# Scaling the second copy of the values on GpSimd instead of VectorE

## The chip, the cores and the metric

The kernel runs on one core of a Trainium2 chip. The core has five engines, each with a queue of its own that it works through in order: TensorE (PE, with its weight loads as PEld), VectorE (DVE), ScalarE (ACT), GpSimd (POOL) and SyncE (SP, which issues DMAs). They wait for one another through semaphores. The metric is the time of one execution on the device, in microseconds (us).

## What is computed

Two branches share one normalised input, and both are added to x:

```python
xn = layernorm(x)                              # x: 1 x 2048 x 512, bf16
# A: attention with 32 heads of 16 columns
q, k, v = split(xn @ wqkv)
p = softmax(q @ k.T * 16 ** -0.5)              # 2048 x 2048 for each head
a = (p @ v) @ wo
# B: an MLP over the token axis
u = gelu(einsum("bsd,sf->bdf", layernorm(xn), w1) + b1)
y = (einsum("bdf,fs->bds", u, w2) + b2).transpose
return x + a + y
```

## The kernel before

The work of attention is cut into 32 blocks: 4 blocks of 512 queries (qb) by 8 groups of 4 heads. For each block, PE makes scores for 16 tiles of 128 keys, 4 heads at once in four row groups of the array, into banks of PSUM (`ps`). The exponential of the scores is made in two ways, tile by tile:

- ScalarE takes the exponential of a bank into `pT` (`exp_tile`, L775).
- Or VectorE turns the score into a 16-bit integer whose bits, read as bf16, are a rough exponential (`first_planes`, L839). Two more such integers, shifted by constants, are derived from it, and the three, read as bf16, are summed by PE to a finer exponential. The three are called planes. The second and third plane are an add of one constant to four 16-bit integers at a time, done by GpSimd as a 64-bit integer add (`make_plane`, L849, `INT64_ADD` in the profile), in a few cases by VectorE. The planes lie in `planes` and, once their first contents are no longer needed, in `x_sb`, `xn_sb`, `xnT` and `w2blk`. One such region is up to four tiles of 512 columns.

The product with the values (`pv_mm`, L787) takes an exponential or a plane as its moving operand and 17 columns for each head of the values as weights: 16 of values and one of ones, which gives the softmax's denominator. The first of the three planes has the weight 0.75 (`WEIGHT[0]`). So the values are held twice: `V17` with the values and the ones, and `V17b`, the same times 0.75, which is used with first planes alone. (The profile's names leave numbers out: `V` is V17, `V17b` stays.)

The values are made in 19 pieces (`v_steps`): one piece of 4 key tiles and six of 2 for the first 8 heads (T = 0), four of 4 key tiles for the next 8 (T = 1), eight of 2 key tiles for the last 16 (T = 2 and 3). For each piece PE multiplies, VectorE copies the result from PSUM into V17 (`v_evac`, L692, `CAST V<-ps`), and `v_scale` (L750) writes the piece of V17b. A piece is 544 columns on 128 partitions, in six cases 272.

The order of all work is written out by hand as a text of codes (`ORDER`) and replayed into one list for each engine; each operation waits for the writers of what it reads and for the readers of what it overwrites. `sc.add("dve", ...)` appends to VectorE's list, `sc.add("pool", ...)` to GpSimd's. The place of a piece's scaling in the text is a few steps behind its copy. Before its first integer add GpSimd has memsets alone: constants, zeros of V17b and of parts of `QT` and `gT`.

## Time and profile before

| | |
|---|---|
| median of 3 runs | 627.7 us (627.61 to 628.27) |
| the profiled execution | 627.96 us, span 626.2 us |
| PE busy | 617.4 us (99%) |
| ACT busy | 614.1 us (98%) |
| DVE busy | 584.3 us (93%) |
| POOL busy | 430.6 us (69%) |
| granted TensorE clock | 1.0 |

The span is the time from the first to the last record of the program on the core; the execution's own time is 1.8 us longer. Busy shares are means over all stages. In the lists below, a row of a queue gives the start and the length in us, the engine, the source line, the operation, what it writes and reads, and in brackets the idle time of the engine ahead of it and who ended it. `x2` is a merged pair of like operations.

### The profile page before, as it was taken

To read this page: it belongs to the slowest core of one execution; us is meant where nothing else is said; L and a number is where in the kernel's file an instruction comes from. 1 tells how busy PE (TensorE), PEld (TensorE's weight loads), DVE (VectorE), ACT (ScalarE), POOL (GpSimd) and SP (SyncE) were. 2 spreads that over 40 slices of the span, in tenths; PEclk is the share of its full clock that TensorE was granted. 3 is DMA by queue.
4 is the path that set the end of the run, shared out by engine and by line. 5 is a ranking of instruction groups with operands and counts; after the bars stand their busy time and mean duration, and the time that the engine had idled before them with its cause. 6 is when DMAs were issued, how large, how long until landed. Compare 5 with 4: busy or idle time off the path is not lost.

```text
span 626.2 us, 20539 instructions
## 1 busy us (share of the span) xinstructions
PE 617.4 (99%) x8776; PEld 195.6 (31%) x8776; DVE 584.3 (93%) x909; ACT 614.1 (98%) x698; POOL 430.6 (69%) x624
## 2 busy tenths in 40 slices
PE   8999999999999999999999999999999999999997
PEld 4544333232222222222323323222222222322222
DVE  6999999989999999999999998998989999999996
ACT  7999999999999999999999999999999999999996
POOL 2105766766767766769789777877867788887784
PEclk9999999999999999999999999999999999999999
DMA  8001210112202122030020031212141022122011
GB/s 236 5 12 40 50 54 6 38 41 54 51 14 63 36 59 48 20 78 13 28 52 24 17 86 41 56 41 74 36 107 35 19 57 47 50 52 68 20 27 45
DMA packets 69530, 29.74 MB, mean 47 GB/s; under 512 B 56198, under 2 KB 66438, under 8 KB 69438
## 3 DMA queue, kind: packets, MB, share of 16 engines
q1 hardware_dynamic: 69006, 28.03, 18.3%
q8 instruction: 69, 1.13, 0.8%
q10 hardware_dynamic: 432, 0.39, 0.2%
q14 instruction: 23, 0.19, 0.1%
HBM read 21.88 MB, written 2.59 MB: 39 GB/s over the span
## 4 chain that ended last, share of the span: by engine, by line
PE 84%; ACT 10%; DVE 5%; issue 0%
PE ps L787 33%; PE ps L762 29%; PE ps L667 21%; ACT pT L775 7%; ACT wqkv_sb L775 3%; DVE x_sb L839 1%; DVE planes L839 1%; PE ps L673 1%; DVE xn_sb L839 1%; DVE xnT L692 0%; DVE xnT L839 0%; PE ps L679 0%; DVE xn_sb L630 0%; DVE stats L604 0%; DVE zer L1078 0%
## 5 line engine op out<-in xcount | busy, mean ns | idle before, releaser
L775 ACT ACTIVATE pT<-ps 128x1024 bf16<-128x1024 f32 (+2 forms) x488 | 459.7, 1033 | 2.1 <-PE ps L762 1.5
L762 PE MATMUL ps<-QT,KT 32*128 32x512 bf16 x2048 | 253.3, 384 | 1.5 <-ACT pT L775 0.4
L839 DVE TENSOR_SCALAR planes<-ps 128x512 int16<-128x512 f32 (+1 forms) x268 | 200.4, 778 | 14.6 <-PE ps L660 6.9
L775 ACT ACTIVATE wqkv_sb<-ps 128x1024 bf16<-128x1024 f32 (+2 forms) x172 | 174.7, 1038 | 0.1
L787 PE MATMUL ps<-pT,V 128*32 128x512 bf16 x950 | 157.7, 386 | 0.6 <-DVE V L692 0.6
L839 DVE TENSOR_SCALAR x_sb<-ps 128x512 int16<-128x512 f32 (+1 forms) x190 | 139.9, 766 | 7.9 <-PE ps L762 3.2
L762 PEld LDWEIGHTS ps<-QT,KT 32*128 32x128 bf16 x2048 | 65.9, 90 | 238.3 <-ACT pT L775 146.6
L787 PE MATMUL ps<-planes,V 128*32 128x512 bf16 x574 | 116.1, 384 | 0.0
L787 PE MATMUL ps<-x_sb,V 128*32 128x512 bf16 x477 | 98.1, 383 | 0.0
L849 POOL INT64_ADD planes<-planes x79 | 60.4, 769 | 43.4 <-DVE planes L839 36.6
L787 PE MATMUL ps<-wqkv_sb,V 128*32 128x512 bf16 x335 | 83.2, 386 | 0.0
L787 PE MATMUL ps<-planes,V17b 128*32 128x512 bf16 x314 | 77.4, 384 | 0.1
L849 POOL INT64_ADD planes<-x_sb x80 | 59.0, 743 | 23.7 <-DVE x_sb L839 22.0
L839 DVE TENSOR_SCALAR xnT<-ps 128x512 int16<-128x512 f32 (+1 forms) x89 | 69.5, 810 | 1.3 <-PE ps L660 0.6
L849 POOL INT64_ADD x_sb<-planes x64 | 52.9, 830 | 20.4 <-DVE planes L839 17.6
L839 DVE TENSOR_SCALAR xn_sb<-ps 128x512 int16<-128x512 f32 (+1 forms) x73 | 58.3, 817 | 4.5 <-PE ps L762 2.9
L787 PE MATMUL ps<-x_sb,V17b 128*32 128x512 bf16 x219 | 56.8, 384 | 0.0
L667 PE MATMUL ps<-gT,w2blk 128*32 128x512 bf16 (+1 forms) x688 | 53.0, 383 | 0.0
L787 PEld LDWEIGHTS ps<-pT,V 128*32 128x32 bf16 x950 | 39.3, 94 | 38.2 <-issue 35.1
L667 PE MATMUL ps<-xn_sb,w1blk 128*32 128x512 bf16 x624 | 50.4, 383 | 0.0
L787 PE MATMUL ps<-xnT,V 128*32 128x512 bf16 x204 | 49.0, 383 | 0.0
L787 PE MATMUL ps<-xn_sb,V 128*32 128x512 bf16 x203 | 43.8, 383 | 0.0
(121 smaller groups left out, 899.5 us busy)
## 6 DMA issues: line engine op xcount, KB each, us to landing
w1blk<-in_B_w_dram SPq DMA_DIRECT2D x10, 512.0 KB
w2blk<-in_B_w_dram SPq DMA_DIRECT2D x16, 320.0 KB
denb<-rec_scr SPq DMA_DIRECT2D x15, 256.0 KB
xres<-in_A_x_dram SPq DMA_DIRECT2D x16, 128.0 KB, 3.1
QT<-qraw SPq DMA_DIRECT2D x120, 16.0 KB, 1.8
OT<-OT SPq DMA_DIRECT2D x60, 32.0 KB, 3.0
out_dram<-osb SPq DMA_DIRECT2D x13, 128.0 KB, 2.2
x_sb<-in_A_x_dram SPq DMA_DIRECT2D x2, 512.0 KB
```

Of the source, the lines that this page charges most:

```text
L667: op = sc.add("pe", lambda e, sl=sl, c=c: e.matmul(dst[sl, :], lhsT=lhsT[:, sl], rhs=rhs, start=start, stop=stop, tile_position=(0, 32 * c ...
L673: return sc.add("pe", lambda e: e.matmul(bank(bk)[:, 0:n], lhsT=zer[:, 512:640], rhs=zer[:, 0:n], start=True, stop=True), reads=[("zer",)] ...
L762: return sc.add("pe", lambda e: e.matmul(bank(bk), lhsT=KT[32 * r:32 * r + 32, T, 128 * kt:128 * (kt + 1)], rhs=QT[32 * r:32 * r + 32, slo ...
L775: return sc.add("act", lambda e: e.activation(slots(us), pick(ps3, bs), ACTF.Exp, scale=EXP_SCALE), reads=[("bank", b) for b in bs], write ...
L787: return sc.add("pe", lambda e: e.matmul(bank(PV_BANK)[32 * r:32 * r + 32, :], lhsT=vt_[:, off:off + 32], rhs=rhs, start=start, stop=stop, ...
L839: return sc.add("dve", lambda e: e.tensor_scalar(pick(plane_i[pb].rearrange("p (r n) -> p r n", n=512), ss), pick(ps3, bs), BIAS + SHIFT[0 ...
L849: return sc.add("pool", lambda e: e.int64_add(plane_q[pb][:, 0:128 * n], plane_q[pb0][:, 0:128 * n], -down * LANES), reads=rd, writes=wr, ...
```

## The change

`v_scale` adds its multiplication to GpSimd's list instead of VectorE's. What it reads, what it writes and its place in the text of codes are the same.

```diff
         def v_scale(t, n_, T0_, T1_):
             dst, src = v_span(V17b, t, n_, T0_, T1_), v_span(V17, t, n_, T0_, T1_)
             keys = [(q, T) for q in range(t, t + n_) for T in range(T0_, T1_)]
-            return sc.add("dve", lambda e: e.tensor_scalar(dst, src, WEIGHT[0], None, ALU.mult),
+            return sc.add("pool", lambda e: e.tensor_scalar(dst, src, WEIGHT[0], None, ALU.mult),
                        [("V", 0, q, T) for q, T in keys] + [("Vone",)], [("V", 1, q, T) for q, T in keys])
```

The order of PE, ACT and SP is the same in both programs; VectorE has 19 operations fewer and GpSimd more. VectorE's queue around the last two scalings ahead of the first integer add, as the difference of the two programs (line, operation, what it writes and reads, partitions by columns):

```order
 L692 CAST V<-ps 128x4x8x16
-L750 TENSOR_SCALAR V17b<-V 128x4x136
 L692 CAST KT<-ps 128x512
 L839 TENSOR_SCALAR planes<-ps 128x512
 L692 CAST V<-ps 128x4x8x16
-L750 TENSOR_SCALAR V17b<-V 128x4x136
 L839 TENSOR_SCALAR planes<-ps 128x512
```

The first planes follow VectorE's copies of the values directly there.

GpSimd's queue before, from its last memset over the first eight integer adds; an `ISA` row with operands is an `INT64_ADD`, and the bare `ISA` row ahead of the first tells GpSimd which set of routines the next operations need:

```order
L520 MEMSET gT 128x512
L849 ISA
L849 ISA planes<-planes 128x1024 x2
L849 ISA w2blk<-planes 128x1024
L849 ISA x_sb<-planes 128x1024 x3
L849 ISA planes<-x_sb 128x1024 x2
```

The same place in the changed program, down to the third bare row of L750:

```order
L520 MEMSET gT 128x512
L750 TENSOR_SCALAR V17b<-V 128x2x136 x5
L750 TENSOR_SCALAR V17b<-V 128x4x136 x2
L849 ISA
L849 ISA planes<-planes 128x1024 x2
L750 ISA
L750 TENSOR_SCALAR V17b<-V 128x4x136
L849 ISA
L849 ISA w2blk<-planes 128x1024
L849 ISA x_sb<-planes 128x1024
L750 ISA
L750 TENSOR_SCALAR V17b<-V 128x4x136
```

Seven scalings come ahead of the first add, and from there on single scalings stand between the adds, each with a bare `ISA` row on either side. In the whole program GpSimd has one such bare row before and 22 after.

## The prediction

> **What bounds the kernel now.** I read the page's first part, then the chain that ended last, then a table of the three early stretches, then GpSimd's (POOL's) queue in order of time over the place of the change.

> The page: its span, its busy shares, and the chain by engine.

> ```profile
> span 626.2 us, 20539 instructions
> PE 617.4 (99%) x8776; PEld 195.6 (31%) x8776; DVE 584.3 (93%) x909; ACT 614.1 (98%) x698; POOL 430.6 (69%) x624
> PE 84%; ACT 10%; DVE 5%; issue 0%
> ```

> TensorE (PE) is the bound: 84% of the chain, and it works through a fixed order. What it loses to a wait anywhere comes back nowhere, since ScalarE (98%) has no room to make it up either. VectorE (DVE), which the change relieves, is 5% of the chain. POOL, which it loads, is not on the chain at all.

> The same by stretch. The second row is the stretch in which the first integer adds and most of the moved work lie (busy us and count, engine by engine):

> ```profile
> core 0: us, PE busy (x) PEld busy (x) DVE busy (x) ACT busy (x) POOL busy (x), PEclk, DMA share, GB/s
> 0.00:49.30 49.30, 45.05 (x974) 22.96 (x974) 42.35 (x123) 44.88 (x76) 6.29 (x52) 1.00 0.29 80
> 49.30:97.10 47.80, 47.80 (x804) 17.85 (x804) 46.63 (x81) 47.74 (x54) 31.81 (x40) 1.00 0.20 48
> ```

> In that stretch POOL is busy 31.81 of 47.80 us, so it has 16.0 us to spare; PE has none.

> **What is removed.** The scalings on DVE, by shape, and the two that come last ahead of the first integer add, with the copy they follow:

> ```profile
> L750 DVE TENSOR_SCALAR V17b<-V 128x544 bf16<-128x544 bf16 x13 | 4.4, 340 | 0.1
> L750 DVE TENSOR_SCALAR V17b<-V 128x272 bf16<-128x272 bf16 x6 | 1.4, 225 | 0.0
> 42.77 0.30 DVE L750 TENSOR_SCALAR V17b<-V 128x544 bf16<-128x544 bf16 x1
> 45.11 0.69 DVE L692 CAST V<-ps 128x512 bf16<-128x512 f32 x1
> ```

> DVE loses 13 x 0.340 + 6 x 0.225 = 5.8 us, all before 97 us. With DVE at 5% of the chain this is worth about 0.3 us (5.8 x 0.05). I count it as nothing.

> **What is added, and its place.** Nineteen TENSOR_SCALARs stand in POOL's queue instead, each waiting for DVE's copy of the values. That is not all. The order of the changed program has 22 bare ISA rows on POOL (11 of L750, 11 of L849) where before there was one. In the built program such a row carries the number of a library of POOL routines: 0 ahead of a TENSOR_SCALAR, 1 ahead of an INT64_ADD. So POOL changes its code whenever it goes from one kind to the other: once at the start, once to the first INT64_ADD, and then in ten pairs, there and back, around ten single scalings among the integer adds.

> POOL's queue before, at those places (start, length, then in brackets the idle time ahead and who ended it). Rows marked x2 are two adds:

> ```profile
> 21.19 0.31 POOL L520 MEMSET V17b<- 128x256 bf16 x1 [16.64 <-DVE xn_sb L630]
> 23.01 0.52 POOL L520 MEMSET gT<- 128x512 bf16 x1
> 49.33 2.05 POOL L849 INT64_ADD planes<-planes  x2 [25.81 <-DVE planes L839]
> 52.53 1.04 POOL L849 INT64_ADD w2blk<-planes  x1 [1.14 <-DVE planes L839]
> 56.03 2.05 POOL L849 INT64_ADD x_sb<-planes  x2 [1.45 <-DVE planes L839]
> 60.17 2.09 POOL L849 INT64_ADD planes<-x_sb  x2 [2.10 <-DVE x_sb L839]
> 64.07 1.04 POOL L849 INT64_ADD w2blk<-planes  x1 [1.81 <-DVE planes L839]
> 67.61 2.05 POOL L849 INT64_ADD x_sb<-planes  x2 [1.48 <-DVE planes L839]
> 70.60 1.63 POOL L849 INT64_ADD planes<-planes  x2 [0.94 <-DVE planes L839]
> 78.74 0.89 POOL L849 INT64_ADD planes<-x_sb  x2
> 82.54 1.20 POOL L849 INT64_ADD planes<-x_sb  x2 [0.55 <-DVE x_sb L839]
> 94.91 1.04 POOL L849 INT64_ADD x_sb<-x_sb  x1 [1.45 <-DVE x_sb L839]
> 95.93 1.19 POOL L849 INT64_ADD planes<-x_sb  x1
> ```

> The one change of code in before stands in the 25.81 us of idle time ahead of 49.33, so its length S is covered there and no row has it.

> Who needs POOL's results: PE's first products with them (weights last in the name).

> ```profile
> 48.90 0.39 PE L787 MATMUL ps<-planes,V17b 128*32 128x512 bf16 x3
> 50.64 0.40 PE L787 MATMUL ps<-planes,V 128*32 128x512 bf16 x3
> 55.03 0.39 PE L787 MATMUL ps<-planes,V 128*32 128x512 bf16 x1
> 83.64 0.38 PE L787 MATMUL ps<-planes,V 128*32 128x512 bf16 x1
> 98.95 0.38 PE L787 MATMUL ps<-planes,V 128*32 128x512 bf16 x2
> ```

> The first of the adds of 49.33 is done at 50.36 and read at 50.64; the adds from 52.53 are read from 55.03; the one of 95.93 is done at 97.12 and read at 98.95. So POOL may be late by 0.3 to 2 us and no more; behind that PE's queue stands still, scores and projections included.

> **One TENSOR_SCALAR on POOL.** No row has it. It lies between POOL's memset of 512 columns (0.52 us, the row of 23.01) and its add over 512 64-bit elements (1.04 us); I take the middle, 0.78. The scaling is over 544 columns in all ten that count, so the ten are worth 5.2 to 10.4 us. The nine earlier ones follow DVE copies that end by 45.80 us, in POOL's idle time (16.64 us ahead of 21.19, 25.81 ahead of 49.33); the memsets behind the first two waited for DVE until 21.19 already. They cost nothing; without that cover they would be at most 7.0 us of POOL. The first reader of the copy comes at 48.90, after all nine. No DMA moves and SP's queue is the same.

> **One change of code, S.** From above it is bounded by the 25.8 us. Below, nothing shows that it costs anything at all; the nearest rows are ScalarE's load of its own table and what any move of bytes takes to land (last number of the DMA rows):

> ```profile
> 1.65 1.28 ACT L570 ACT_TABLE_LOAD   x1 [1.65 <-PEq L1360]
> QT<-qraw SPq DMA_DIRECT2D x120, 16.0 KB, 1.8
> x_sb<-in_A_x_dram SPq DMA_DIRECT2D x2, 256.0 KB, 5.1
> ```

> [...]

> [...]

> **The sum.** I lay POOL's queue out anew. The last early scaling starts when DVE's copy ends, at 45.11 + 0.69 = 45.80, and ends at 46.58; the code changes until 46.58 + S; the first add stood at 49.33. It is late by S - 2.75. Each of the ten pairs then adds 2S + 0.78, less the idle time that POOL had ahead of the group behind it, because by then PE and DVE, which POOL now keeps waiting, have delivered: 1.14, 1.45 + 2.10 (three adds stand between those two without a change of code), 0, 1.81, 1.48, 0.94, 0, 0.55, 1.45 and 0, in sum 10.92. In the groups of several adds without a change of code (70.6 to 78.7 and 82.5 to 93.5) I leave the small waits as they were. At the end:

> S - 2.75 + 10 x (2S + 0.78) - 10.92 = 21 S - 5.9.

> PE may take the last of these results 98.95 - 97.12 = 1.8 us late, which leaves 21 S - 7.7. With S = 6.8 this is 142.8 - 7.7 = 135.1 us. After that stretch POOL holds adds alone, and everything runs as before, 135 us later. The profiled execution took 627.96 us (span 626.2 and 1.8 around it), 0.26 above the median of 627.7; 627.96 + 135.1 = 763.1, against the median 762.8. I forecast 763 us.

> [...]

> **Rivals.**

> 1. *The change of code is free*, because both sets stay on the engine; this ends on the other side. For it: no DMA queue of the page grows in the 25.8 us, and nothing in before shows a price. Against it: the program was built to ask for it every time. Then a pair is 0.78 us, and the idle times and PE's slack hold it everywhere (the tightest place is 82.54, with 0.55 idle ahead and about 0.5 us from the first add's end, 82.54 + 0.60, to its reader at 83.64). The time is 627.7 less DVE's 0.3: 627.4, no change. It decides where 2S + 0.78 is under about 1.0, so for S under 0.1.

> 2. *It costs like ScalarE's table load*, 1.28 us: 21 x 1.28 - 7.7 = 19 us, 647. For it: the one row of an engine that reloads what it computes with. [...] Up to S = 5.0 (725) I put here.

> 3. *It is much dearer*, on the way to the 25.8: at S = 12 it is 21 x 12 - 7.7 = 244 us, 872. [...] Against it: the longest landing is 5.1.

> **How the numbers follow.** Forecast (S of 5.0 to 8.8) 0.78; free 0.05; cheap, up to 5.0, 0.08; dear, over 8.8, 0.09. S = 5.0 gives 97.3 us and 725; S = 8.8 gives 177.1 and 805; with the uncertainty of the scaling (2.6 us) and of the clock inside it the range is 725 to 805. Of the free case 0.03 is within 0.2% (1.3 us, about what a measurement of this kernel can tell) and 0.02 faster; all else is slower, 0.95.

> **What would show it.** Right: POOL's idle time between 46 and 230 us comes in gaps of about S on both sides of each TENSOR_SCALAR; its first INT64_ADD stands at about 53 us and the add of 95.93 at about 233; PE waits for POOL's planes some 130 us in all and is at 81% (617 of 761); after the last pair, stretches are as long as before; TENSOR_SCALAR on POOL 0.5 to 1.1 us. Wrong: gaps near zero beside TENSOR_SCALAR, a PE that isn't stopped there, or time lost after the last pair, where POOL's queue is unchanged.

## The result, and the profile after

The changed kernel takes 767.45 us (764.8 to 768.42) against 627.7 us: 1.2217 times the time before by the means of the runs, 95% interval 1.2202 to 1.2232. The forecast was 763, in a range of 725 to 805. The profiled execution took 768.32 us, 140.4 more than the one before.

The page after: span, busy shares, the span in 40 slices for PE, POOL and the granted clock, and the chain by engine.

```profile
span 766.5 us, 20580 instructions
PE 639.1 (83%) x8776; PEld 197.5 (26%) x8776; DVE 582.8 (76%) x890; ACT 617.6 (81%) x698; POOL 456.7 (60%) x643
...
PE   8984341152806999999999999999999999999998
...
POOL 2331221242324757767676969777687687787875
PEclk9996666575866999999999999999999999999999
...
PE 68%; issue 13%; ACT 8%; DVE 7%; POOL 4%; POOLq 0%; DVEq 0%
```

From the fourth slice to the twelfth PE is idle most of the time (but for the ninth and the eleventh), and so is POOL, which PE waits for. 13% of the chain is "issue", time in which the engine waited for nothing that the profile shows. From slice 14 on the picture is that of before.

By stretch, the middle one from the first integer add to the end of the last pair:

```profile
core 0: us, PE busy (x) PEld busy (x) DVE busy (x) ACT busy (x) POOL busy (x), PEclk, DMA share, GB/s
0.00:49.30 49.30, 44.77 (x981) 22.68 (x981) 41.77 (x115) 45.41 (x76) 16.63 (x61) 1.00 0.29 80
49.30:240.00 190.70, 72.37 (x847) 21.23 (x844) 49.74 (x78) 54.67 (x58) 49.60 (x52) 0.64 0.05 12
```

The middle stretch holds 847 matmuls in 190.7 us, where before 804 took 47.8. PE, the busiest engine, is at work for 38% of it (72.37 us), and the DMAs are nearly idle (0.05).

POOL's queue in that stretch, some of its rows (the brackets give the idle time ahead):

```profile
45.37 1.57 POOL L750 TENSOR_SCALAR V17b<-V 128x544 bf16<-128x544 bf16 x1 [1.42 <-DVE V L692]
52.77 2.05 POOL L849 INT64_ADD planes<-planes  x2 [5.83 <-issue]
61.74 1.61 POOL L750 TENSOR_SCALAR V17b<-V 128x544 bf16<-128x544 bf16 x1 [6.92 <-issue]
69.10 1.03 POOL L849 INT64_ADD w2blk<-planes  x1 [5.75 <-issue]
70.12 1.03 POOL L849 INT64_ADD x_sb<-planes  x1
78.80 1.61 POOL L750 TENSOR_SCALAR V17b<-V 128x544 bf16<-128x544 bf16 x1 [7.65 <-DVE x_sb L839]
...
192.93 1.20 POOL L849 INT64_ADD planes<-x_sb  x2 [5.72 <-issue]
...
203.54 2.05 POOL L849 INT64_ADD planes<-x_sb  x2 [1.02 <-DVE x_sb L839]
...
220.50 1.03 POOL L849 INT64_ADD x_sb<-x_sb  x1 [6.00 <-issue]
228.29 1.61 POOL L750 TENSOR_SCALAR V17b<-V 128x544 bf16<-128x544 bf16 x1 [6.76 <-issue]
235.73 3.06 POOL L849 INT64_ADD planes<-x_sb  x3 [5.84 <-issue]
```

Every time the queue goes from a TENSOR_SCALAR to an INT64_ADD or back, POOL stands still. Eleven gaps lead to an INT64_ADD, 5.72 to 6.13 us, in sum 64.7 (mean 5.88); ten lead to a TENSOR_SCALAR among the adds, 6.74 to 7.65 us, in sum 71.05 (mean 7.1). Between two adds there is no such gap. A few gaps are put down to DVE, as the row of 78.80; its length is that of the others, and DVE's copy was long there (it ended at 57.24).

At the start of such a gap the trace has short records. Under line 750 it has 22 named MODIFY_POOL_CONFIG, two for each of the eleven bare `ISA` rows (shortest, median and longest in ns). Below that row are three pieces of the chain that ended last, from the first scaling among the adds to the next add (`POOLq` is POOL's queue, here with such a record of line 849):

```profile
L750 POOLq MODIFY_POOL_CONFIG  x22: 1/1/12, 4.6 to 221.6; - x22
...
63.57 0.01 POOLq L849
...
63.61 5.49 issue
69.10 1.04 POOL w2blk L849
```

The record ahead of the add is 0.01 us long; the 5.49 us between it and the add have no record of their own, so what POOL does in them is not shown. A change of code below stands for a bare `ISA` row of the program with the gap behind it.

What PE's weight loads waited for on POOL, the three largest rows (total, times, longest). In before the same three are 1.8, 3.4 and 0.5 us, never more than 0.3 at a time:

```profile
PEld ps L787 <- POOL planes L849: 73.3, 17, 15.1
...
PEld ps L787 <- POOL x_sb L849: 42.3, 22, 14.3
...
PEld ps L787 <- POOL w2blk L849: 17.8, 4, 10.7
```

That is 133.4 us of waiting for planes, up to 15.1 at a time; two changes of code and one scaling are 14.6 (5.9 + 7.1 + 1.6). And nothing comes back later. The same add and the same last store, in before and then in after:

```profile
128.87 1.63 POOL L849 INT64_ADD x_sb<-xnT  x2 [0.30 <-DVE xnT L839]
...
623.54 0.45 SPq L516 DMA_DIRECT2D out_dram<-xres  x1
```

```profile
269.19 1.62 POOL L849 INT64_ADD x_sb<-xnT  x2 [0.30 <-DVE xnT L839]
...
763.90 0.45 SPq L516 DMA_DIRECT2D out_dram<-xres  x1
```

The add is 140.32 us later, the store 140.36.

### The profile page after: what moved, and what is told of

Its sections match the earlier page's. It is cut to its first block, busy times and chain, and to the rows that moved or that the text cites. A ratio compares the mean times of both kernels' runs of the same rounds, so it can differ in the third digit from the quotient of the medians.

```text
span 766.5 us, 20580 instructions
## 1 busy us (share of the span) xinstructions
PE 639.1 (83%) x8776; PEld 197.5 (26%) x8776; DVE 582.8 (76%) x890; ACT 617.6 (81%) x698; POOL 456.7 (60%) x643
## 2 busy tenths in 40 slices
DMA packets 69530, 29.74 MB, mean 39 GB/s; under 512 B 56198, under 2 KB 66438, under 8 KB 69438
## 3 DMA queue, kind: packets, MB, share of 16 engines
q1 hardware_dynamic: 69006, 28.03, 15.1%
## 4 chain that ended last, share of the span: by engine, by line
PE 68%; issue 13%; ACT 8%; DVE 7%; POOL 4%; POOLq 0%; DVEq 0%
PE ps L787 27%; PE ps L762 23%; PE ps L667 17%; ACT pT L775 6%; ACT wqkv_sb L775 2%; DVE planes L839 2%; POOL V17b L750 2%; DVE x_sb L839 2%; POOL planes L849 1%; DVE xn_sb L839 1%; POOL x_sb L849 1%; DVE V L692 0%; DVE stats L604 0%; PE ps L679 0%; DVE xnT L839 0%
## 5 line engine op out<-in xcount | busy, mean ns | idle before, releaser
L762 PE MATMUL ps<-QT,KT 32*128 32x512 bf16 x2048 | 258.2, 393 | 1.5 <-ACT pT L775 0.4
L839 DVE TENSOR_SCALAR planes<-ps 128x512 int16<-128x512 f32 (+1 forms) x268 | 200.4, 776 | 55.9 <-PE ps L762 38.7
L839 DVE TENSOR_SCALAR x_sb<-ps 128x512 int16<-128x512 f32 (+1 forms) x190 | 140.1, 765 | 64.1 <-PE ps L762 47.5
L787 PE MATMUL ps<-planes,V 128*32 128x512 bf16 x574 | 120.0, 398 | 66.8 <-POOL planes L849 66.8
L787 PE MATMUL ps<-pT,V 128*32 128x512 bf16 x950 | 162.9, 398 | 0.6 <-DVE V L692 0.6
L787 PE MATMUL ps<-x_sb,V 128*32 128x512 bf16 x477 | 101.7, 398 | 34.7 <-POOL x_sb L849 34.7
L750 POOL TENSOR_SCALAR V17b<-V 128x544 bf16<-128x544 bf16 (+1 forms) x19 | 26.5, 1394 | 100.8 <-issue 49.3
L849 POOL INT64_ADD planes<-x_sb x80 | 58.7, 738 | 42.4 <-issue 23.7
L787 PE MATMUL ps<-wqkv_sb,V 128*32 128x512 bf16 x335 | 83.2, 386 | 0.0
L787 PE MATMUL ps<-planes,V17b 128*32 128x512 bf16 x314 | 80.7, 398 | 0.1
L849 POOL INT64_ADD planes<-planes x79 | 60.3, 768 | 28.5 <-issue 11.8
L839 DVE TENSOR_SCALAR xnT<-ps 128x512 int16<-128x512 f32 (+1 forms) x89 | 69.4, 808 | 1.3 <-PE ps L660 0.6
L849 POOL INT64_ADD x_sb<-planes x64 | 52.8, 829 | 29.1 <-DVE planes L839 14.7
L839 DVE TENSOR_SCALAR xn_sb<-ps 128x512 int16<-128x512 f32 (+1 forms) x73 | 58.3, 816 | 4.5 <-PE ps L762 2.9
L787 PE MATMUL ps<-x_sb,V17b 128*32 128x512 bf16 x219 | 59.7, 395 | 0.0
L787 PEld LDWEIGHTS ps<-planes,V 128*32 128x32 bf16 x574 | 29.0, 96 | 86.5 <-POOL planes L849 72.8
L839 DVE TENSOR_SCALAR w2blk<-ps 128x512 int16<-128x512 f32 (+1 forms) x26 | 18.4, 744 | 42.2 <-PE ps L762 42.0
## 6 DMA issues: line engine op xcount, KB each, us to landing
denb<-rec_scr SPq DMA_DIRECT2D x15, 256.0 KB
```

Of the source, the lines that this page charges most:

```text
L750: return sc.add("pool", lambda e: e.tensor_scalar(dst, src, WEIGHT[0], None, ALU.mult), [("V", 0, q, T) for q, T in keys] + [("Vone",)], [ ...
L762: return sc.add("pe", lambda e: e.matmul(bank(bk), lhsT=KT[32 * r:32 * r + 32, T, 128 * kt:128 * (kt + 1)], rhs=QT[32 * r:32 * r + 32, slo ...
L787: return sc.add("pe", lambda e: e.matmul(bank(PV_BANK)[32 * r:32 * r + 32, :], lhsT=vt_[:, off:off + 32], rhs=rhs, start=start, stop=stop, ...
L839: return sc.add("dve", lambda e: e.tensor_scalar(pick(plane_i[pb].rearrange("p (r n) -> p r n", n=512), ss), pick(ps3, bs), BIAS + SHIFT[0 ...
L849: return sc.add("pool", lambda e: e.int64_add(plane_q[pb][:, 0:128 * n], plane_q[pb0][:, 0:128 * n], -down * LANES), reads=rd, writes=wr, ...
```

## The experiments

Theory A says that the time goes into the changes of POOL's code. Rival B puts it into the work itself, which POOL does more slowly than DVE, or into the two hindering each other.

**The same work on POOL, without a change of code.** A plain copy stands in the place of each scaling; the factor 0.75 is left out.

```diff
-            return sc.add("pool", lambda e: e.tensor_scalar(dst, src, WEIGHT[0], None, ALU.mult),
+            return sc.add("pool", lambda e: e.tensor_copy(dst, src),
```

> All nineteen pieces of V17b are written on GpSimd from V17 as in the changed kernel, but by a plain copy instead of a multiplication (the factor 0.75 is left out), so that GpSimd's queue has one bare ISA row as before and not 22. Theory A, the time goes into the changes of code: 627.4 to 629 us; the copies (0.5 to 1.6 us each) fit into GpSimd's idle time, and at most the tightest place (0.55 us idle, 0.5 us until the reader) costs some tenths. Rival B, the time goes into GpSimd's slow elementwise work on all pieces, or into VectorE and GpSimd hindering each other: ten copies among the adds still hold TensorE up, 640 us or more.

Measured: 627.75 us, ratio 0.9998 (0.9989 to 1.0007). Its copies, and two rows of its queue:

```profile
L750 POOL COPY V17b<-V 128x544 bf16<-128x544 bf16 x13 | 8.3, 640 | 16.3 <-DVE V L692 16.2
...
51.27 0.64 POOL L750 COPY V17b<-V 128x544 bf16<-128x544 bf16 x1
52.45 1.04 POOL L849 INT64_ADD w2blk<-planes  x1 [0.54 <-DVE planes L839]
```

The copy goes between the adds with no gap, and the add behind it still waits for DVE. The nineteen pieces on POOL and DVE's relief of 5.8 us together change nothing that can be measured. The copies take 0.64 us where the scaling takes 1.6, so this run alone does not yet clear the scaling's own length.

**The changes of code, without the work.** All scalings are on DVE; at the ten late places POOL multiplies one column into a scratch tile.

```diff
+        scr = sb("scr", [128, 2], BF16)
 ...
+            if not (T0_ == 0 or (t, T0_) in ((0, 1), (4, 1))):
+                sc.add("pool", lambda e: e.tensor_scalar(scr[:, 0:1], src[:, 0, 0:1], WEIGHT[0], None, ALU.mult),
+                       [("V", 0, q, T) for q, T in keys] + [("Vone",)], [("scr",)])
-            return sc.add("pool", ...
+            return sc.add("dve", ...
```

> All nineteen scalings are on VectorE as in the kernel before; in addition GpSimd multiplies one column of each of the ten last pieces into a scratch tile that nobody reads, at the places where the changed kernel scales. The ten pairs of changes of code stay, GpSimd's 1.6 us of work at each is nearly gone, and the first change is covered as before. Theory A: the first add is on time (3.4 us less than in the changed kernel) and each pair is about 1.45 us shorter: 767.5 - 3.4 - 14.5 = 750 us (745 to 755). Rival B, the scaling's own work on GpSimd is the cost: 627.7 to 635 us.

Measured: 753.75 us (752.33 to 755.34), ratio 1.2017 (1.1997 to 1.2037).

```profile
L752 POOL TENSOR_SCALAR scr<-V 128x1 bf16<-128x1 bf16 x10 | 2.6, 263 | 72.0 <-issue 64.8 <-DVE planes L843 7.2
```

2.6 us of work, with 72.0 us of gaps ahead of it (7.2 each, as in the changed kernel), cost 126 of the 140 us. So the changes of code are nine tenths of the loss, and B falls as its main cause. The work has the smaller part: ten scalings of 1.61 us in place of 0.26 are 13.5 us, and the first add, 3.4 us late in the changed kernel, is on time here. These 16.9 us stand against 13.7 between the medians and 16.0 between the profiled executions.

**Half of the pairs.** The nine early scalings and every second late one stay on POOL.

```diff
+            eng = "dve" if (t, T0_) in ((12, 1), (2, 2), (6, 2), (10, 2), (14, 2)) else "pool"
-            return sc.add("pool", ...
+            return sc.add(eng, ...
```

> The nine early scalings and every second of the ten later ones (key tiles 8-11 of the second eight heads, 0, 4, 8 and 12 of the last sixteen) stay on GpSimd, the five between are back on VectorE: five pairs of changes of code instead of ten. Theory A: 3.2 us for the first add, 5 x (6.9 + 1.6 + 5.9) = 72 less 4.1 us of idle time that is used up and 1.8 us until the last reader: 69 us, 697 us (690 to 704), half of the whole loss. Rival C, most of the loss comes from a few of the places, or from TensorE's lowered clock in a lasting state: off that line by more than 10 us.

Measured: 699.6 us (699.14 to 700.01), 71.9 more than before, half of 139.75 within 2 us. That is inside the range of theory A (690 to 704), and rival C falls: the loss goes with the number of changes.

**One pair alone.**

```diff
+            eng = "pool" if (t, T0_) == (8, 1) else "dve"
-            return sc.add("pool", ...
+            return sc.add(eng, ...
```

> One scaling alone (key tiles 8 to 11, second eight heads, at 51.5 us before) is on GpSimd, so there is one pair of changes of code, between the first adds; the other eighteen are on VectorE. Theory A: 6.9 + 1.6 + 5.8 us from 51.4, so the adds of 52.5 stand at about 65.7, 13.2 late, of which their reader forgives 1.5: 11.7 us longer, and up to 2 us for TensorE's lowered clock after the wait: 639.4 to 641.5 us. Rival B: 1.6 us of work against 1.1 us idle and 1.5 us until the reader: 627.7 us.

Measured: 642.26 us, ratio 1.0226 (1.0212 to 1.024). POOL's queue, the one wait of PE for it, three stretches around, and two products of PE behind the wait:

```profile
49.33 2.05 POOL L850 INT64_ADD planes<-planes  x2 [25.80 <-DVE planes L840]
58.36 1.61 POOL L751 TENSOR_SCALAR V17b<-V 128x544 bf16<-128x544 bf16 x1 [6.98 <-issue]
66.04 1.03 POOL L850 INT64_ADD w2blk<-planes  x1 [6.07 <-issue]
...
PE ps L788 <- POOL w2blk L850: 12.0, 1, 12.0
...
62.00:66.00 4.00, 0.00 (x0) 0.00 (x0) 0.00 (x0) 0.00 (x0) 0.00 (x0) 0.50 0.00 0
66.00:70.00 4.00, 2.87 (x20) 0.49 (x20) 0.63 (x1) 0.67 (x1) 3.96 (x4) 0.50 0.02 4
70.00:80.00 10.00, 10.00 (x176) 4.05 (x176) 8.83 (x16) 9.02 (x11) 3.88 (x5) 0.93 0.04 10
...
67.13 0.61 PE L788 MATMUL ps<-planes,V 128*32 128x512 bf16 x1
...
71.93 0.39 PE L763 MATMUL ps<-QT,KT 32*128 32x512 bf16 x3
```

The first add is on time: a change of code ahead of it is covered by 25.80 us of idle time. The pair makes PE wait 12.0 us, and the time is 14.4 longer, 0.8 above the range that was expected. The rest goes with the clock: it is 0.50 while nothing runs, and still 0.50 for 4.3 us in which PE works again (67.13 to 71.4, by the mean of 0.93 in the last stretch). The products of 67.13 and 71.93 stood at 55.03 and 57.67 before: 12.1 us late at the start of that work and 14.3 behind it, with PE busy throughout, so the lowered clock costs 2.2 us.

**Changes of code that have time.** First only the seven scalings of T = 0 on POOL, then eight, then all nine that come ahead of the first add. (Two of the nine stand ahead of GpSimd's last memsets, so the list of the changed program further up, which begins behind those, shows seven.)

```diff
+            eng = "pool" if T0_ == 0 else "dve"                               # seven
+            eng = "pool" if T0_ == 0 or (t, T0_) in ((0, 1),) else "dve"      # eight
+            eng = "pool" if T0_ == 0 or (t, T0_) in ((0, 1), (4, 1)) else "dve"   # nine
-            return sc.add("pool", ...
+            return sc.add(eng, ...
```

> Only the seven scalings of the first eight heads stay on GpSimd; the twelve others are back on VectorE. GpSimd changes its code twice, at 4 us and at about 39 us. Theory A: the second change (about 5.8 us, as in the changed kernel's gaps ahead of adds) ends at about 45 us, ahead of the first add at 49.3, so it is covered: 627.4 to 628.0 us, no difference. Rival B: seven scalings of 0.9 to 1.6 us in an idle engine: no difference either, unless the two engines hinder each other, then a few tenths more. Both see no gain from VectorE's 1.9 us of freed time.

> The ninth early scaling (key tiles 4 to 7 of the second eight heads) is on VectorE too, so GpSimd's last early scaling ends at about 44.1 us instead of 47.1 and the change of code at about 49.9. Theory A: the first add is 0.5 us late, its reader forgives 0.3, TensorE's wait is too short to lower its clock: 627.9 us (627.6 to 628.4), no difference that can be told. Rival, a change of code costs some us whether or not GpSimd has time for it: 630 us or more.

> The nine scalings ahead of the first integer add stay on GpSimd, the ten among the adds are back on VectorE. Theory A: the change of code can start only after the ninth scaling, at about 47 us, so the first add stands at about 52.8 instead of 49.3 us and its reader had 0.3 us: 3.2 us longer, 630.9 us (630 to 632). Rival B: nine scalings in idle time, 627.7 us.

Measured: seven 627.95 us (ratio 1.0000, 0.9991 to 1.0009); eight 629.03 (1.0022, 1.0013 to 1.0031); nine 634.38 (1.0101, 1.0088 to 1.0115). The first add of each, in that order:

```profile
49.46 2.06 POOL L850 INT64_ADD planes<-planes  x2 [9.71 <-DVE planes L840]
```

```profile
50.05 2.05 POOL L850 INT64_ADD planes<-planes  x2 [5.94 <-DVE planes L840]
```

```profile
52.86 2.05 POOL L850 INT64_ADD planes<-planes  x2 [5.79 <-issue]
```

With 9.71 us between the last scaling and the add, the two changes of code cost nothing. With eight the add is 0.7 us late and the kernel 1.3 longer. That is above the expected 627.6 to 628.4: of the 1.3, 0.6 stands in the trace up to the last store (issued at 624.10 us instead of 623.54); the rest lies behind that store (span 627.5 us against 626.2), and its reason stays open. With nine the add is 3.5 us late, but the kernel is 6.6 us longer, 2.4 over the range that was expected.

**Where the rest of the nine's loss goes.** PE waits for the first add there, once, and then runs on a lowered clock:

```profile
PE ps L788 <- POOL planes L850: 3.3, 1, 3.3
...
54.00:58.00 4.00, 4.00 (x80) 2.16 (x80) 1.68 (x3) 2.04 (x2) 2.42 (x3) 0.50 0.00 0
58.00:62.00 4.00, 4.00 (x47) 0.94 (x47) 2.59 (x5) 2.50 (x4) 0.55 (x1) 0.71 0.00 0
62.00:66.00 4.00, 4.00 (x78) 1.57 (x78) 3.70 (x6) 4.00 (x5) 2.05 (x2) 1.00 0.66 141
```

It can also be that ScalarE and VectorE run dry in the wait and need time to get back into step. To tell the clock from that, the wait was filled with products of zeros added to the open sums of the product with the values:

```diff
+        filled = []
 ...
+                        if not filled and sc.last_writer[item[b, kt, r, j][1]].eng == "pool":
+                            filled.append(1)
+                            rows = [q for q in range(4) if n_done.get((b, q)) is False]
+                            assert len(rows) == 4
+                            for _ in range(14):
+                                zero_rows(PV_BANK, rows, [], False)
                         rhs, key, which = item.pop((b, kt, r, j))
```

> As the run with nine early scalings (634.4 us, of which 3.3 us are TensorE's wait for the first integer add and TensorE's granted clock is 0.5 for 6.8 us behind it), but TensorE fills that wait with 56 products of zeros (14 groups of four, about 3.1 us) that add nothing to the sums. Theory D, the 3.3 us beyond the wait are the clock that falls when TensorE stands still: the clock stays at 1.0 and the time is 631.0 us (630.6 to 631.8). Rival E, they are the engines' loss of step after any wait (ScalarE and VectorE run dry): 634 us or more, with the clock at 1.0 all the same.

Measured: 632.12 us (631.74 to 632.6), ratio 1.0067 (1.0055 to 1.008).

```profile
50.18 3.41 PE L1162 MATMUL ps<-zer 128*32 128x512 bf16 x56
...
54.00:58.00 4.00, 4.00 (x104) 1.86 (x104) 2.93 (x6) 3.05 (x4) 2.93 (x3) 1.00 0.01 4
```

The add is as late as before (52.83 us), the clock stays at 1.00, and 104 matmuls go through the stretch in which it was 80 without the filling. The time is 0.3 above the range of theory D and well under the 634 of rival E. So 2.3 us of the 6.6 (634.38 - 632.12) are the clock's. What is left is 4.4 us against the 3.3 that PE is held up; in the trace the last add of the stretch (60.17 before, 63.44 here) is 3.3 later and the whole span 3.6, so about 1 us is not explained, as in the run with eight.

## Why the prediction was right

The mechanism is the one forecast: the runs with work and no change of code, and with changes and next to no work, part the two, and the run with half of the pairs and the one with a single pair follow the count of changes. That the size came out so near has luck in it, as the first two points below say. By the terms of the sum, from the trace after:

| term | forecast us | measured us |
|---|---|---|
| first add late | 4.05 (S - 2.75) | 3.44 (52.77 - 49.33) |
| twenty changes of code in ten pairs | 136.0 (20 x 6.8) | 129.9 (71.05 + 58.85) |
| ten scalings | 7.8 | 16.1 |
| idle time used up | -10.9 | -9.6 (what is left over) |
| last add late | 136.9 | 139.8 (235.73 - 95.93) |
| last reader's patience, clock | -1.8 | +0.6 (-1.9 + 2.5) |
| whole | 135.1 | 140.4 |

- **The price of a change, S.** No run shows the 6.8 that the sum uses; it was an estimate of the author's, the geometric middle of two far ends, 1.8 us (the shortest DMA landing) and 25.8 us (the idle time that covered the one change before). Over the 21 gaps it is 6.46 ((64.7 + 71.05) / 21): 5.88 ahead of INT64_ADD, 7.1 ahead of TENSOR_SCALAR. That the middle lay so near is luck: nothing in the profile before held the number. Nor does any run show that DMA landings have a part in it: the page counts 69530 DMA packets and 29.74 MB in both programs, although the second changes its code 21 times more. For the same reason the quiet DMA queues of before, which rival 1 had on its side, said nothing.
- **One scaling on POOL was mis-sized**: 0.78, between bounds of 0.52 and 1.04, from a memset and an integer add. It takes 1.61 us over 544 columns, outside the 0.5 to 1.1 that was named as a sign. Both bounds came from other kinds of instruction, and an instruction of the same queue with as many columns did not bound it. The two errors, 6.1 us too much for the changes in the pairs and 8.3 too little for the work, nearly cancel, which is luck too.
- **Idle time.** That the waits ahead of a group disappear behind a change of code holds: no group that follows one has any wait beyond the change. In the groups of several adds the waits were left as they were, and grew instead: 82.54 to 93.46 became 192.93 to 205.59 (203.54 + 2.05), 1.7 us more. PE's clock is 0.50 at the start of that group; whether that is the reason was not tried.
- **The last reader's patience** of 1.8 us held, and the clock then took more than that. Three stretches of the changed kernel, from the last pair on, then PE's first product with the last add's result and a later one of scores; the last row is that later one in before:

```profile
235.70:240.00 4.30, 3.19 (x23) 0.67 (x23) 1.41 (x3) 1.02 (x1) 3.06 (x3) 0.50 0.00 0
240.00:244.00 4.00, 4.00 (x40) 0.86 (x37) 2.50 (x4) 2.61 (x3) 2.05 (x2) 0.62 0.00 0
244.00:250.00 6.00, 6.00 (x81) 1.73 (x78) 5.82 (x11) 6.00 (x8) 3.88 (x5) 1.00 0.05 12
...
236.81 0.61 PE L787 MATMUL ps<-planes,V 128*32 128x512 bf16 x2 [14.20 <-POOL planes L849]
243.01 0.39 PE L762 MATMUL ps<-QT,KT 32*128 32x512 bf16 x3
...
102.65 0.39 PE L762 MATMUL ps<-QT,KT 32*128 32x512 bf16 x3
```

The first product stood at 98.95 before, so PE is 137.9 us late there, 1.9 less than the add. From then on PE is busy without a break, at a clock of 0.50 until 243.0, and is 140.4 us late at the second product: what took 3.7 us takes 6.2. So the lowered clock costs 2.5 us at this place, and nothing comes on top later. The sum has no term for the clock: before, its mean was 1.000, and what the range allows for it was the author's guess, which nothing in the profile before shows.

- **DVE's relief** was counted as nothing; the copies on POOL agree (0.9998). **The early changes** were to be covered: the seven show it at the start; ahead of the first add the change was forecast not to be covered, and is not.
- **Rivals.** The free change, the change like ScalarE's table load, and the change at 8.8 us and more are excluded by the gaps themselves.

## What to carry to other kernels

Before an operation is moved to GpSimd, look in the built order for bare ISA rows. In this kernel, where such a row stood at every alternation between TENSOR_SCALAR and INT64_ADD, each pair cost two gaps, means 7.1 and 5.88 us (7.2 ahead of a TENSOR_SCALAR of one column), and the loss went with the count of pairs: 71.9 us with five, 139.75 with ten. A change with 9.7 us of idle time around it was free, and with 5.9 us the kernel was 1.3 us longer, so keep each kind together, or use an operation that has no such row (the plain copy here, 627.75 us). An engine with 31% idle time on the whole page had 16 us to spare in the stretch that mattered, and the engine that bounds the kernel forgave it 0.3 to 1.9 us at the places that were looked at.
